# Reordering decodes, low parts, left sums and x differences at the end of the first block of a fused retention and two-layer kernel

## The chip, the cores and the metric

The kernel runs on one core of one Trainium2 chip. The metric is the device time of one execution in microseconds (us). The kernel before takes 845.2 us, the median of 3 runs (844.39 to 845.39).

## The reference

```python
def _attn_ref(q, k, v):                    # (4, 8, 576, 64) each
    scores = (1.0 / np.sqrt(D_)) * np.matmul(q, k.transpose(0, 1, 3, 2))
    Dmat = np.where(rel >= 0, gamma[:, None, None] ** rel[None, :, :], 0.0)
    return np.matmul(scores * Dmat[None, :, :, :], v)

x = attn_out.transpose(0, 2, 1, 3).reshape(B * S, H * D)      # 2304 x 512
h = x @ moe_w_in                                              # 512 x 2048
x = np.maximum(h, 0.0) ** 2 @ moe_w_out                       # 2048 x 512
h = x @ moe2_w_in
out = (h * np.clip(h + 3.0, 0.0, 6.0) / 6.0) @ moe2_w_out
```

The weights arrive as 64 bit floats. The kernel keeps close to float32 accuracy by splitting each operand into a rounded high part and a low part (the rest), and by doing three products (high by high, high by low, low by high) for one.

## The kernel before

**Stages.** The retention comes first (up to about 64 us). Then the first layer works on three blocks of 768 tokens and the second layer on three more. The first block of the first layer is special: it runs over 16 chunks of 128 hidden columns, loop `for c in range(NCH)` (L940), and on the way turns all the weights of layer 1 from 64 bit words to float32 and splits them. The five other blocks run as `NPAIR * len(BLOCKS)` = 40 pairs of chunks (L1022), in which `pair` (L675) makes the hidden part of two chunks with seven products of half size (P1 to P7, in the order P1, P6, P2, P7, P5, P4, P3; a Strassen scheme) in place of eight. The seven products take seven right operands, made of x and of differences of x, and left operands made of the weights and of sums of them.

**One chunk c of the first block** (L940 to L1003). TensorE does `emit_h(c)` (L423: 24 matmuls into PSUM banks 6 and 7), and at the chunk's end `firsts(c - 2)` (24 matmuls with the hidden values of two chunks ago). The other engines do, each in the order of the program:

- `decode` (L155) of one half of a weight chunk: two ScalarE passes (L171, L172, "first"), then VectorE's `clamp` (L175, L178), `second` (L184) and `third` (L190). In chunk c those of the output weights `wd` of chunk c-1 and of the input weights `w` of chunk c+2; in chunk 14 the two are the output weights of 13 and of 14.
- `emit_g(c)` (L459): ReLU, square and high part on ScalarE (L447, L450, L451) for both halves, then the two low parts on VectorE (L454).
- `split_out` (L404) and `split_in` (L395): high part on ScalarE (L196), low part on GpSimd (L197).
- in odd chunks `sum_lefts` (L936): the left sums of a pair, four VectorE subtractions and additions (L508 to L511), and their store, which is queued in `late_stores` and issued by `store_late` (L499) on SP.
- `next_load` (L769): the next load of weights, on SP, which waits until VectorE has read the old contents of its buffer (L184).

**The border to the pairs.** `operand_steps` (L568) gives three lists for the next block: `sums`, eight VectorE differences of x, two for each of T1, T2, T3 and T4 (L585); `highs` (L602, ScalarE) and `lows` (L607, VectorE), a high and a low part of each of the seven right operands. `parts_of_left` (L635) gives the high and low part of a left operand (L196 on ScalarE, L197 on VectorE), `load_left` (L613) loads one pair's left operands on SP. In the kernel before T1, T2, T3 stand at the end of chunks 11, 12, 13; `highs[0]` at the end of 13; `highs[1]`, `lows[0]` and two high parts of left operands at the end of 14; in chunk 15, ahead of `emit_g(15)`, `lows[1]`, two low parts of left operands and the last `sum_lefts`. After the loop come `highs[2]` to `lows[4]` (L1006 to L1011), the late stores, the stores of two output weights, and `load_left(1)`. T4 stands after P1 of the first pair (L1047), ahead of the addition `add(u2, tb, p1)` (L729; the instruction is L714), which must have read bank `b1` before P7 may write it (L735).

**Slots.** `ready_slots` (L527) spreads the decoding and splitting of layer 2's weights over 119 slots, which `between(i)` of the pairs takes one by one (L1060): seven per pair, none in the last pair of a block, three in the first pair of a later block. One period of 14 slots serves one pair of chunks: sums on GpSimd (L508 to L511) may go as soon as the decode in slot 6 is done, left operands are split in slots 8, 11, 14 and 17 (that of slot 11 is half as wide, 128x256).

Of the kernel before, what the change touches and what calls it, by code (L numbers as in the profile page):

```python
# [74 lines left out]
def retention_moe_moe2(ctx, tc, qk, qk_last, kv, w_in, w_out, w_in2, w_out2, consts, out):  # L75
# [6 lines left out]
    NCH = DFF // 128  # L82
# [694 lines left out]
    with tc.manual_schedule():  # L777
# [153 lines left out]
        def firsts(c):  # L931
            return ywork(wouts[c], g[c], c == 0, c == NCH - 1)

        left_lows = []

        def sum_lefts(p):  # L936
            whole = left_sums(*(first_in[p][:, e] for e in range(2)), nc.vector)[1]
# [2 lines left out]
        for c in range(NCH):  # L940
            mine, p = wins[c], c // 2
            h = emit_h(c)
            dec, due = due, []
            if c < 2:
                opening(c, h, dec)
                dec = []
            first = dec[:1]
            dec = dec[len(first):]
            for d in first:
                for f in d:  # L950
                    f()
                next_load()
            for d in dec:
                d.pop(0)()
            if c == NCH - 1:
                lows[1]()
                for f in left_lows:
                    f()
                sum_lefts(p)
            if c > 1:  # L960
                emit_g(c, h)
            for d in dec:
                for f in d:
                    f()
                next_load()
            if c in (2, 3):
                load()
            store_late()
            for n, w in ((c, mine), (c + 1, wins.get(c + 1))):
                if w is not None and (n != c or not c):  # L970
                    keep(("s", 0, n // 2, n % 2), w.rearrange("p a b n -> p (a b n)"), slice(n % 2, 2))
            if 2 <= c < NCH - 1:
                split_out(c - 1, nc.gpsimd)
            if c >= NCH - 2:
                split_out(c, nc.gpsimd)
            while halves and halves[0][0] <= c:
                due.append(decode(*halves.pop(0)[1:]))
            for d in due[:1]:
                d.pop(0)()
            if c and c + 2 < NCH:  # L980
                split_in(c + 2)
            if c % 2 and c < NCH - 1:
                sum_lefts(p)
            for d in due[1:]:
                d.pop(0)()
            if c >= LAG:
                for f in firsts(c - LAG):
                    f()
                keep(("o", 0, c - LAG), wouts[c - LAG].rearrange("p e n -> p (e n)"))
            if c == NCH - 5:  # L990
                load_left(0)
            if NCH - 5 <= c < NCH - 2:
                for f in sums[2 * (c - NCH + 5):][:2]:
                    f()
            if c == NCH - 3:
                highs[0]()
            if c == NCH - 2:
                highs[1]()
                lows[0]()
                for e in (2, 3):  # L1000
                    high, low = parts_of_left(0, e)
                    high()
                    left_lows.append(low)  # L1003
        assert not halves and not due
        pending = firsts(NCH - 2) + firsts(NCH - 1)
        highs[2]()  # L1006
# [1 line left out]
        lows[2]()  # L1008
        highs[4]()
        lows[3]()  # L1010
        lows[4]()  # L1011
        store_late()
        for c in (NCH - 2, NCH - 1):
            keep(("o", 0, c), wouts[c].rearrange("p e n -> p (e n)"))
# [7 lines left out]
        for k in range(total):  # L1022
# [20 lines left out]
            if p == 0:  # L1043
                if j:
                    side[0].append(lows[4])
                else:
                    side[0] += sums[6:]  # L1047
                for i, at in ((5, 1), (6, 3)):
                    side[at].append(highs[i])
                    side[at + 1].append(lows[i])  # L1050
            for i, e in ((4, 1), (6, 0)):
# [5 lines left out]
                    for n in range(2):  # L1057
                        side[i + n].append(lambda e=e, n=n: parts_of_left(k + 1, e)[n]())
            if p < NPAIR - 1:
                for i in range(4 if j and not p else 0, 7):  # L1060
                    if slots:
                        side[i] += [store_late] + slots.pop(0)
            elif late_stores:
# [54 lines left out]
```

## Time and profile before

| what | value |
|---|---|
| median of the runs | 845.2 us (844.39 to 845.39) |
| profiled execution, its own time | 845.26 us |
| span of the profiled execution | 843.5 us |
| TensorE (PE) busy | 825.0 us, 98% |
| VectorE (DVE) busy | 586.1 us, 69% |
| ScalarE (ACT) busy | 466.6 us, 55% |
| GpSimd (POOL) busy | 144.5 us, 17% |
| granted TensorE clock | 0.999, at the upper level throughout |

The span runs from the first to the last instruction; 1.76 us lie around it. A row of the timeline gives the start in us from the span's start, the duration in us, the engine, the line of the kernel, the operation, output and inputs, how many instructions are merged in the row, and in brackets the idle time of the engine before it with what ended it.

### The profile page before, as it was taken

The numbers are of one execution on the slowest core, as the hardware profiler recorded it, in microseconds if no ns is written. First come the engines' busy times: TensorE is split into PE (matmuls) and PEld (weight loads), VectorE is DVE, ScalarE is ACT, GpSimd is POOL, SyncE is SP. The second block draws the span as 40 slices with busy tenths as digits, with TensorE's granted clock in tenths as the row PEclk, the third lists the DMA queues.
The fourth block names the chain that finished last, engine by engine and source line by source line (L and its number), as shares of the span: only waits on it lengthen the run. The fifth ranks groups of instructions, "written<-read, shape, count | busy, mean of one in ns | idle before, by whom it ended". The sixth has DMA issues, their size and how long they took to land.

```text
span 843.5 us, 14173 instructions
## 1 busy us (share of the span) xinstructions
PE 825.0 (98%) x5220; PEld 741.9 (88%) x5220; DVE 586.1 (69%) x1018; ACT 466.6 (55%) x913; POOL 144.5 (17%) x122
## 2 busy tenths in 40 slices
PE   8989999997999999999999999999999999999998
PEld 7878888886999899999999888898898888889886
DVE  5779999999787876887875895546644546534434
ACT  1248777768865876867775653335433345433332
POOL 2353333331332320132230130000000000000000
PEclk9999999999999999999999999999999999999999
DMA  9996788876787894689786688553854552854522
GB/s 364 343 300 221 239 289 282 294 249 242 258 326 275 304 330 177 232 280 362 276 293 266 225 287 312 202 185 137 316 221 163 188 199 87 329 209 161 201 99 75
DMA packets 77963, 206.58 MB, mean 245 GB/s; under 512 B 8005, under 2 KB 24773, under 8 KB 77895
## 3 DMA queue, kind: packets, MB, share of 16 engines
q1 hardware_dynamic: 77314, 204.90, 68.9%
q8 instruction: 41, 0.67, 0.3%
q10 hardware_dynamic: 580, 0.79, 0.3%
q14 instruction: 28, 0.22, 0.1%
HBM read 159.00 MB, written 46.66 MB: 244 GB/s over the span
## 4 chain that ended last, share of the span: by engine, by line
PE 80%; DVE 7%; DMA 6%; ACT 4%; issue 1%; SPq 1%; POOL 0%; DVEq 0%; ACTq 0%; POOLq 0%
PE hps L690 33%; PE yps L650 22%; PE yps L478 13%; PE ytail L478 7%; PE hps L431 5%; DMA kvt<-in_kv_dram 3%; DMA qkt<-in_qk_dram 3%; DVE a L184 1%; DVE g L454 1%; DMA stage<-in_w_out_dram 1%; DVE w L190 1%; DVE a L178 1%; ACT u L706 0%; ACT r L172 0%; DVE u L714 0%
## 5 line engine op out<-in xcount | busy, mean ns | idle before, releaser
L650 PE MATMUL yps<-wo,g 128*128 128x512 f32 x864 | 226.8, 394 | 1.5 <-DVE g L710 1.3
L690 PE MATMUL hps<-xlast,win 128*128 128x384 f32 x960 | 194.9, 338 | 1.7 <-DVE u L714 1.6
L650 PEld LDWEIGHTS yps<-wo,g 128*128 128x128 f32 x864 | 159.4, 188 | 26.0 <-DVE g L710 2.0
L690 PEld LDWEIGHTS hps<-xlast,win 128*128 128x128 f32 x960 | 167.7, 188 | 10.5 <-DVE u L714 2.1
L714 DVE TENSOR_TENSOR u<-hps,u 128x384 f32<-128x384 f32 x120 | 66.8, 557 | 157.1 <-PE hps L690 150.5
L478 PE MATMUL yps<-g,wo 128*128 128x512 f32 x576 | 166.1, 396 | 0.4 <-POOL wo L197 0.4
L690 PE MATMUL hps<-xop,win 128*128 128x384 f32 x720 | 146.4, 338 | 3.7 <-ACT r L447 3.4
L690 PEld LDWEIGHTS hps<-xop,win 128*128 128x128 f32 x720 | 125.7, 188 | 10.7 <-ACT r L447 3.6
L708 ACT ACTIVATE g<-c 128x384 fp32r<-128x384 f32 x120 | 63.1, 525 | 88.1 <-DVE c L707 86.6
L478 PEld LDWEIGHTS yps<-g,wo 128*128 128x128 f32 x576 | 101.8, 188 | 10.2 <-POOL wo L197 0.8
L478 PEld LDWEIGHTS ytail<-g,wo 128*128 128x128 f32 x576 | 94.0, 188 | 17.3
L478 PE MATMUL ytail<-g,wo 128*128 128x256 f32 x576 | 98.5, 279 | 0.0
L710 DVE TENSOR_TENSOR g<-c,g 128x384 fp32r<-128x384 f32 x120 | 67.9, 566 | 11.3 <-ACT g L708 11.1
L431 PE MATMUL hps<-xring,win 128*128 128x512 f32 (+1 forms) x384 | 69.7, 338 | 0.3 <-ACT r L447 0.2
L733 ACT ACTIVATE c<-hps 128x384 f32<-128x384 f32 x40 | 19.7, 492 | 90.9 <-PE hps L690 90.9
L431 PEld LDWEIGHTS hps<-xring,win 128*128 128x128 f32 x384 | 60.1, 190 | 8.7 <-ACT r L447 0.7
L706 ACT ACTIVATE u<-c,three 128x384 f32<-128x384 f32 x72 | 44.4, 617 | 31.7 <-DVE c L714 30.5
L714 DVE TENSOR_TENSOR c<-hps,u 128x384 f32<-128x384 f32 x80 | 44.3, 554 | 21.8 <-PE hps L690 21.7
L184 DVE SCALAR_TENSOR_TENSOR a<-stage,a 128x512 int32<-128x512 int32 x64 | 51.2, 800 | 0.9
L707 DVE SCALAR_TENSOR_TENSOR c<-u,c 128x384 f32<-128x384 f32 x72 | 41.3, 574 | 13.5 <-ACT u L706 13.4
L171 ACT ACTIVATE a<-stage 128x512 f32<-128x512 f32 x64 | 42.4, 663 | 6.4 <-DMA stage<-in_w_in_dram 6.4
L172 ACT ACTIVATE r<-stage 128x512 int32<-128x512 uint32 x64 | 42.2, 660 | 0.0
(97 smaller groups left out, 905.5 us busy)
## 6 DMA issues: line engine op xcount, KB each, us to landing
win<-kept SPq DMA_DIRECT2D x88, 512.0 KB
wo<-kept SPq DMA_DIRECT2D x80, 512.0 KB
kept<-ready SPq DMA_DIRECT2D x40, 512.0 KB
win<-kept SPq DMA_DIRECT2D x72, 256.0 KB
stage<-in_w_out_dram SPq DMA_DIRECT2D x32, 512.0 KB
kept<-wo SPq DMA_DIRECT2D x16, 512.0 KB
stage<-in_w_in_dram SPq DMA_DIRECT2D x16, 512.0 KB
qkt<-in_qk_dram SPq DMA_DIRECT2D x13, 512.0 KB
```

Source lines behind the costliest of these rows:

```text
L171: nc.scalar.activation(out=a, in_=high.bitcast(F32), func=ACTF.Abs)
L172: nc.scalar.activation(out=r, in_=low.bitcast(U32), func=ACTF.Copy, scale=2.0 ** -29)
L184: nc.vector.scalar_tensor_tensor(out=a.bitcast(I32), in0=high, scalar=-0x40000000, in1=a.bitcast(I32), op0=ALU.bitwise_and, op1=ALU.bitwis ...
L431: nc.tensor.matmul(out=h, lhsT=w[:, kk // 2, wp, kk % 2 * 128:][:, :128], rhs=xs[kk][xp][:, o:o + n], start=m == 0, stop=m == 3 * KD - 1,)
L478: nc.tensor.matmul(out=p, lhsT=w[:, wp, m * 128:m * 128 + 128], rhs=gt[:, gpart, o:o + n], start=first and e == 0 and not (k and m % 2), s ...
L650: nc.tensor.matmul(out=p, lhsT=gt[:, gpart, m * 128:m * 128 + 128], rhs=w[:, wp], start=first and e == 0, stop=last and e == 2,)
L690: nc.tensor.matmul(out=to, lhsT=wl[k][:, half if k != 1 else 0, wp, o], rhs=x[:, xp, f], start=first and m == 0, stop=last and m == 5, ski ...
L706: nc.scalar.activation(out=v, in_=c, func=ACTF.Relu, bias=three)
L707: nc.vector.scalar_tensor_tensor(out=c, in0=v, scalar=6.0, in1=c, op0=ALU.min, op1=ALU.mult)
L708: nc.scalar.activation(out=hi, in_=c, func=ACTF.Copy)
L710: lambda: nc.vector.tensor_tensor(out=lo, in0=c, in1=hi.bitcast(F32), op=ALU.subtract)
L714: nc.vector.tensor_tensor(out=out_, in0=to, in1=x, op=ALU.add)
```

## The change

It moves work in the first block and at its border; nothing is added or left out.

- In chunk 14 the rest of the decode of the output weights of 14 (`second`, `third`) and the load behind it go ahead of `emit_g(14)`.
- In chunk 15 one low part of a left operand is left there (that of operand 2); the one of operand 3 and the last `sum_lefts` go behind `lows[4]`, after the loop, and its store with them. The high part of operand 3 goes behind `lows[3]`.
- In chunk 13 `highs[0]` goes ahead of `split_in(15)`.
- T1, T2, T3 go to the ends of chunks 4, 6 and 8.
- In the first pair T4 goes from after P1 to after P6 (behind the addition L729), `highs[5]` and `lows[5]` one place later, and the slots of that pair begin at its place 3 in place of 0, so that all later slots come three places later.

```diff
-        left_lows = []
...
+            if c == NCH - 2:
+                for d in dec:
+                    for f in d:
+                        f()
+                    next_load()
+                dec = []
             if c == NCH - 1:
                 lows[1]()
-                for f in left_lows:
-                    f()
-                sum_lefts(p)
+                left[0][1]()
             if c > 1:
                 emit_g(c, h)
...
+            if c == NCH - 3:
+                highs[0]()
             if c and c + 2 < NCH:
                 split_in(c + 2)
...
-            if NCH - 5 <= c < NCH - 2:
-                for f in sums[2 * (c - NCH + 5):][:2]:
+            if c in (4, 6, 8):
+                for f in sums[c - 4:][:2]:
                     f()
-            if c == NCH - 3:
-                highs[0]()
             if c == NCH - 2:
                 highs[1]()
                 lows[0]()
-                for e in (2, 3):
-                    high, low = parts_of_left(0, e)
-                    high()
-                    left_lows.append(low)
+                left = [parts_of_left(0, e) for e in (2, 3)]
+                left[0][0]()
...
         lows[3]()
+        left[1][0]()
         lows[4]()
+        left[1][1]()
+        sum_lefts(NPAIR - 1)
         store_late()
...
                 else:
-                    side[0] += sums[6:]
-                for i, at in ((5, 1), (6, 3)):
+                    side[1] += sums[6:]
+                for i, at in ((5, 1 if j else 2), (6, 3)):
...
-                for i in range(4 if j and not p else 0, 7):
+                for i in range(0 if p else 4 if j else 3, 7):
```

## Rows read from the trace of the kernel before

**Rows 1.** The page: busy time of the engines, and two of its costliest groups.

```profile
PE 825.0 (98%) x5220; PEld 741.9 (88%) x5220; DVE 586.1 (69%) x1018; ACT 466.6 (55%) x913; POOL 144.5 (17%) x122
...
L650 PE MATMUL yps<-wo,g 128*128 128x512 f32 x864 | 226.8, 394 | 1.5 <-DVE g L710 1.3
...
L710 DVE TENSOR_TENSOR g<-c,g 128x384 fp32r<-128x384 f32 x120 | 67.9, 566 | 11.3 <-ACT g L708 11.1
```

**Rows 2.** Timeline of TensorE, 155 to 215 us: the rows with idle time.

```profile
181.98 4.45 PE L431 MATMUL hps<-xring,win 128*128 128x512 f32 x24 [0.21 <-ACT r L447]
...
187.26 0.50 PE L478 MATMUL yps<-g,wo 128*128 128x512 f32 x1 [0.37 <-POOL wo L197]
...
194.70 1.31 PE L690 MATMUL hps<-xop,win 128*128 128x384 f32 x6 [3.43 <-ACT r L447]
...
203.27 1.32 PE L690 MATMUL hps<-xlast,win 128*128 128x384 f32 x6 [1.56 <-DVE u L714]
```

**Rows 3.** Timeline of ScalarE in chunks 14 and 15.

```profile
188.95 0.63 ACT L196 ACTIVATE wo<-wd 128x512 fp32r<-128x512 f32 x1 [3.62 <-DVE wd L190]
...
191.43 1.13 ACT L196 ACTIVATE win<-win 128x512 fp32r<-128x512 f32 x2
...
194.28 0.37 ACT L447 ACTIVATE r<-hps 128x256 f32<-128x256 f32 x1
```

**Rows 4.** Timeline of VectorE from chunk 14 to the first pair.

```profile
182.21 0.41 DVE L175 TENSOR_SCALAR a<-a 128x512 f32<-128x512 f32 x1
...
185.38 2.11 DVE L454 TENSOR_TENSOR g<-r,g 128x512 fp32r<-128x512 f32 x2
...
190.18 1.12 DVE L175 TENSOR_SCALAR a<-a 128x512 f32<-128x512 f32 x1 [0.32 <-ACT a L171]
...
201.73 1.01 DVE L585 TENSOR_TENSOR xall<-xall,t 128x384 f32<-128x384 f32 x2
202.67 0.55 DVE L714 TENSOR_TENSOR u<-hps,u 128x384 f32<-128x384 f32 x1
```

**Rows 5.** Timeline of VectorE: its first instruction of chunk 4 and of chunk 10.

```profile
95.71 0.41 DVE L175 TENSOR_SCALAR a<-a 128x512 f32<-128x512 f32 x1
...
145.81 0.42 DVE L175 TENSOR_SCALAR a<-a 128x512 f32<-128x512 f32 x1
```

**Rows 6.** Timeline of all engines, 153 to 158 us: a GpSimd operation and two L184.

```profile
153.23 1.31 POOL L197 TENSOR_TENSOR win<-w,win 128x512 fp32r<-128x512 f32 x1 [2.40 <-ACT win L196]
153.27 1.81 DVE L184 SCALAR_TENSOR_TENSOR a<-stage,a 128x512 int32<-128x512 int32 x1
...
157.63 0.69 DVE L184 SCALAR_TENSOR_TENSOR a<-stage,a 128x512 int32<-128x512 int32 x1
```

**Rows 7.** Timelines of TensorE (hidden matmuls of chunks 4, 10) and ScalarE (ReLU of 9).

```profile
89.43 4.34 PE L431 MATMUL hps<-xring,win 128*128 128x512 f32 x24
...
139.71 4.34 PE L431 MATMUL hps<-xring,win 128*128 128x512 f32 x24
...
137.46 0.59 ACT L447 ACTIVATE r<-hps 128x512 f32<-128x512 f32 x1
```

**Rows 8.** SP's and ScalarE's timelines at the first pair; DMA rates, 195 to 220 us.

```profile
198.09 0.32 SPq L412 DMA_DIRECT2D kept<-sums  x1
...
203.46 1.06 SPq L621 DMA_DIRECT2D win<-kept  x2
...
209.36 0.62 ACT L196 ACTIVATE win<-win 128x512 fp32r<-128x512 f32 x1
...
GB/s 0 26 13 0 0 0 315 413 406 406 393 419 400 393 197 302 354 252 318 400 216 315 360 387 406 426 419 419 419 403 390 403 390 370 356 218 39 0 26 0
```

**Rows 9.** Timeline of all engines in the second layer, around a wait of TensorE.

```profile
501.13 0.73 POOL L197 TENSOR_TENSOR ready<-wd,ready 128x256 fp32r<-128x256 f32 x1 [7.18 <-ACT ready L196]
501.17 1.10 DVE L710 TENSOR_TENSOR g<-c,g 128x384 fp32r<-128x384 f32 x1
...
502.32 0.73 PE L650 MATMUL yps<-wo,g 128*128 128x512 f32 x2 [0.97 <-DVE g L710]
```

## The prediction

> **What bounds the kernel now.** I read the page first: TensorE is busy for 98% of the span [rows 1], so a reordering can only win back what TensorE still waits. Its timeline comes next, for the rows with idle time [rows 2]. From 77 to 181 us there is none. Then come four: 0.21, 0.37, 3.43 and 1.56, together 5.57 us, at the first matmuls of chunk 15, at the output matmuls of chunk 13, at P1 of the first pair and at its P7. That is all that the border can give. The rows name the releasers: the ReLU of chunk 15 for P1, the addition L714 for P7. So the third view is what those two engines did before. ScalarE stood idle 3.62 us until the decode of the output weights of 14 was through, and only afterwards came to that ReLU at 194.28 [rows 3]. VectorE has next to no idle time from chunk 14 (182.21) to L714 (202.67): the largest is 0.32 [rows 4]. P7 therefore starts when VectorE has worked off its list, and P1's wait is a wait that P7 would have later anyhow.
>
> **Was VectorE full earlier, too?** This decides the moved differences of x. From chunk 4 to chunk 10 VectorE's start moves by 145.81 - 95.71 = 50.10 us in three periods of two chunks, 16.70 each [rows 5]. TensorE's start moves by 139.71 - 89.43 = 50.28, 16.76 each [rows 7]. From chunk 10 to 14 VectorE takes 182.21 - 145.81 = 36.40 [rows 4, 5], that is two periods and 3.0 more, and in between stand exactly T1, T2 and T3. One pair of differences costs 202.67 - 201.73 = 0.94 [rows 4], three 2.82. So each difference pushed VectorE back by its whole length: there was no gap to fill.
>
> A GpSimd operation is part of that list. L184 takes 0.69 alone and 1.81 when a GpSimd operation has started 0.04 ahead of it [rows 6]: 1.12 lost, four times in two chunks. The Trainium skill, SBUF — State Buffer, section "SBUF: two separate sides", has the two engines share a port pair as an exclusive lock, which whoever starts first holds for the whole instruction, against VectorE operations in a two-port mode or with two SBUF inputs; by it L184 would wait, as here, and an addition that reads PSUM would not. By that rule the lost time can't be ordered away, only handed from one instruction to another.
>
> **The change, part by part.**
>
> - *T1, T2, T3 to chunks 4, 6, 8.* VectorE regains 16.76 - 16.70 = 0.06 us per two chunks, some 0.2 from chunk 8 to 14. So it comes to chunk 14 at about 182.2 as before. I take 0 for this part; the bounds are 0 and -2.8 (if the chunks do hide the three). On the way VectorE is late by 0.94, 1.88, 2.82 us. The ReLU of chunk 9 ends at 137.46 + 0.59 = 138.05, and chunk 10's matmuls need that bank at 139.71 [rows 7]: 1.66 us in hand. TensorE would wait there, about 0.3 at the matmuls of chunk 10 and some 1.2 in all by chunk 12. These waits come out of the border's, since the end is VectorE's.
> - *The decode of 14 ahead of the low parts.* The two low parts take 2.11, of which 1.12 is the lock [rows 4, 6], which will now fall on the decode instead; so the decode ends 0.99 earlier. One high part of a left operand less ahead of the ReLU gives half of 1.13 [rows 3], 0.56. P1 can come at 194.70 - 1.55 = 193.15. VectorE's own list gets no shorter by it, except for the 0.32 that it waited for ScalarE [rows 4]. Against that, the GpSimd operation which overlapped that idle time cost 1.12 - 0.41 = 0.71 there [rows 4], and now has its full 1.12: +0.41.
> - *highs[0] ahead of split_in(15), last left sums and one left low part late.* They stay ahead of L714, so P7 sees the same sum; ScalarE does the high part while it waits for the weights. 0.
> - *T4 behind the addition.* The only work that leaves VectorE's list ahead of L714: -0.94. It is then ahead of the next addition, which needs P7 (1.2 us later) anyway; `highs[5]` and P4 come over 3 us later.
> - *The store of the last sums.* It is issued when the sums are done, some 4 us later than 198.09 [rows 8], and SP holds the output stores and `load_left(1)` behind it. Its third part was issued at 203.46 and is first read at 209.36 [rows 8]. From the store on, 2.5 MB are moved to the end of that part, 6.2 us at the 0.4 MB per us that the row of rates shows [rows 8]: landed at about 209.0, needed at 208.6. ScalarE would wait 0.4, and about 1 us there is covered by the low parts that VectorE has yet to do. 0, bounds 0 and +1.0. The Trainium skill, SBUF — State Buffer, section "The DMA setup-cost knee (why "@ 1 MiB" ≠ asymptote)", gives each transfer about 2 us on top of its bytes, mostly until completion is confirmed; by that the part lands at 211, ScalarE waits 2.4, and the sum would be higher by an estimated 1.4 less what VectorE covers. The rows here don't show a landing, so the sum goes without it.
> - *Slots three places later.* In the second layer VectorE works on the path between the pairs: TensorE waits there for L710 for 1.3 us in all [rows 1], 0.97 of it in one place, where L710 takes 1.10 because a GpSimd low part began 0.04 ahead of it [rows 9]; on average it takes 0.57 [rows 1]. Three places later, the slot that falls there holds the wide low part instead of the 128x256 one, with the four sums shortly before it. Whether L710 or GpSimd is first is a matter of 0.2 us. Bounds: -1.3 (both waits go) and +2.7 (four sums and the wider part each add 0.53, as 1.10 - 0.57). Nearest is the row of today, so 0.
>
> **The sum.** -0.94 - 0.32 + 0.41 = -0.85. The profiled execution has 845.26, its median is 845.2, so one count serves for both: 844.4. A measurement of this kernel can tell about 0.2% (1.7 us) from no change, so this is no difference.
>
> **The rivals.**
>
> *The chunks hide the three differences.* TensorE had no idle time in chunks 3 to 13 and 1.66 us in hand at the ReLU. If VectorE catches up (a lock that falls into idle time), it comes to chunk 14 2.8 us earlier, P1's wait goes altogether, and P7 gains 2.8 + 0.85 of the 5.57: 841.6. Against it stand 16.70 of 16.76 us and the 3.0 us above. 28%.
>
> *Slots collide with the low parts between the pairs of layer 2.* This one ends on the other side. Its place is the end of the first and third pair of the second layer; it decides when GpSimd's operation starts ahead of L710. At +2.7 from the bounds above, with the border's -0.85, it gives 847.1. For it: today's 0.97 with a narrower part. Against it: in the first layer the same slots stand at two other places of the pair with no wait of TensorE for L710, and a wider high part starts GpSimd 0.2 us later, behind L710. 20%.
>
> *P1 is released, P7 is not.* The change does what it says at P1 (1.55 earlier) and all of it comes back at P7. This is my forecast, 52%; its own range is 843.2 to 845.8 (T4 alone and the late loads at either end).
>
> **How the numbers follow.** Faster by over 0.2% (below 843.5): 0.25 of the first rival and 0.05 of the forecast's lower end, 0.30. Slower (above 846.9): 0.16 of the second, with 0.01 from late loads, 0.17. The rest, 0.53, is no difference. The range leaves out about half of the first rival, below 841.6, and the top of the second, above 847.0.
>
> **What would show it.** In the changed kernel's timeline: VectorE's start of chunk 14 at 182 (the first rival: at 179.5); new waits of TensorE by the matmuls of chunks 10 to 12, about 1.2 us; P1 at about 193.2; L714 and P7 at about 201.8 and 202.4, with a wait of over 2 us ahead of P7; two waits for L710 in the second layer, as now or longer. The forecast is wrong if P7 comes before 201, or if TensorE's waits after 210 us exceed 2.5.

## The result and the profile after

The changed kernel takes 850.96 us (median of 7 runs) where the kernel before takes 844.84 beside it: ratio 1.0075, 95% interval 1.0057 to 1.0092. It is 6.1 us slower; the forecast was 844.4.

The page of the changed kernel, busy time and the groups that wait (its profiled execution took 849.28 us, span 847.5):

```profile
PE 829.4 (98%) x5220; PEld 742.9 (88%) x5220; DVE 588.1 (69%) x1018; ACT 465.4 (55%) x913; POOL 141.7 (17%) x122
...
L650 PE MATMUL yps<-wo,g 128*128 128x512 f32 x864 | 227.3, 394 | 1.8 <-DVE g L710 0.8
...
L690 PE MATMUL hps<-xop,win 128*128 128x384 f32 x720 | 146.7, 338 | 4.8 <-ACT u L725 2.3
...
L710 DVE TENSOR_TENSOR g<-c,g 128x384 fp32r<-128x384 f32 x120 | 66.7, 555 | 11.5 <-ACT g L708 10.8
```

TensorE's waits for L710, which the forecast watched, went down from 1.3 [rows 1] to 0.8. In their place stand 2.3 us of waits for L725, the copy of a pair's first product, which the page of before doesn't have. And TensorE is busy 4.4 us longer with the same 5220 matmuls: some of the waiting is inside rows that count as busy. At 469.14 three output matmuls take 1.04 us, with a weight load that waits 0.29 for L710, and 0.86 without; and the clock fell, as shown below.

The timeline of TensorE, its rows with idle time around the border and in the first pairs of layer 2:

```profile
190.90 1.33 PE L690 MATMUL hps<-xop,win 128*128 128x384 f32 x6 [1.73 <-ACT r L447]
...
195.71 1.31 PE L690 MATMUL hps<-xop,win 128*128 128x384 f32 x6 [0.31 <-ACT u L725]
...
200.00 1.65 PE L690 MATMUL hps<-xlast,win 128*128 128x384 f32 x6 [1.93 <-DVE u L714]
...
474.03 1.31 PE L690 MATMUL hps<-xop,win 128*128 128x384 f32 x6 [1.01 <-ACT u L725]
...
487.42 0.73 PE L650 MATMUL yps<-wo,g 128*128 128x512 f32 x2 [0.35 <-DVE g L710]
...
502.72 1.31 PE L690 MATMUL hps<-xop,win 128*128 128x384 f32 x6 [0.64 <-DVE c L714]
...
504.58 0.49 PE L650 MATMUL yps<-wo,g 128*128 128x512 f32 x1 [0.55 <-ACT g L708]
...
505.56 0.73 PE L650 MATMUL yps<-wo,g 128*128 128x512 f32 x2 [0.48 <-DVE g L710]
...
509.17 1.33 PE L690 MATMUL hps<-xop,win 128*128 128x384 f32 x6 [0.45 <-ACT u L725]
```

P1 is at 190.90 and P7 at 200.00, both early on the clock of the page, but the first chunk's matmuls began at 61.33 here and at 63.82 before: attention took 2.5 us less in this one execution. So the border is read from that start on. P1: 129.57 now, 130.88 before. P7: 138.67 now, 139.45 before. The border gained 0.78 at P7, as forecast. From there on it was lost.

The timeline of VectorE (first instruction of chunks 4, 10 and 14, then the addition and T4, which changed places):

```profile
93.26 0.41 DVE L175 TENSOR_SCALAR a<-a 128x512 f32<-128x512 f32 x1
...
146.34 0.41 DVE L175 TENSOR_SCALAR a<-a 128x512 f32<-128x512 f32 x1
...
179.72 0.41 DVE L175 TENSOR_SCALAR a<-a 128x512 f32<-128x512 f32 x1
...
199.39 0.55 DVE L714 TENSOR_TENSOR u<-hps,u 128x384 f32<-128x384 f32 x1
199.86 1.02 DVE L585 TENSOR_TENSOR xall<-xall,t 128x384 f32<-128x384 f32 x2
```

Chunk 4 to 10 takes 53.08 us, where it took 50.10 [rows 5]: 2.98 more for the three differences. Chunk 10 to 14 takes 33.38, where it took 36.40 [rows 4, 5]. From 4 to 14 both kernels take 86.5. Moving the differences moved VectorE's delay and nothing else.

On the way TensorE was held, but not by the ReLU that the forecast named. What it waited for from 130 to 185 us (total, times, longest), where the kernel before has no such row:

```profile
PEld yps L478 <- POOL wo L197: 1.6, 4, 0.7
```

These are the weight loads of the output matmuls, which wait for GpSimd's low part of the output weights. That follows ScalarE's high part, which waits for the decode (L190) on the delayed VectorE.

The windows of five us behind P7's wait; PEclk is the last column but two:

```profile
195.00:200.00 5.00, 2.76 (x17) 2.22 (x15) 4.97 (x13) 1.15 (x3) 0.00 (x0) 1.00 0.00 0
200.00:205.00 5.00, 5.00 (x19) 4.69 (x20) 2.38 (x6) 3.88 (x8) 0.00 (x0) 0.66 0.95 343
205.00:210.00 5.00, 5.00 (x30) 4.60 (x29) 4.97 (x11) 3.54 (x7) 0.00 (x0) 1.00 0.97 323
```

After three waits (1.73, 0.31 and 1.93 us) the granted clock fell. TensorE was busy all of the second five us and did 19 matmuls in them; in the next five it did 30.

To find the 6 us I cut each profile into pieces that don't depend on when the first chunk started. The start of a pair is its first P1 matmul in TensorE's timeline; all are counted from the first chunk's first matmul. A pair without any wait takes 15.85 us in layer 1 (pairs 0 to 15; pair 16 too) and 15.69 in layer 2 (from pair 17 on). The table has all the profiles of this study, the experiments of the next section among them. The kernel before took 844.2 to 845.9 in the rounds that it ran beside the others, so the ratios are compared rather than the medians:

| profile | pair 2 starts at | pairs 2 to 16 | pairs 17 to 19 | median of its runs, ratio [95%] |
|---|---|---|---|---|
| before | 164.91 | 239.12 | 48.97 | 844.84 |
| before2 | 165.11 | 240.15 | 48.99 | one run |
| before3 | 164.92 | 240.48 | 49.14 | one run |
| after | 166.13 | 240.63 | 52.70 | 850.96, 1.0075 [1.0057, 1.0092] |
| after2 | 166.48 | 241.90 | 52.71 | one run |
| s0 | 166.05 | 239.78 | 49.05 | 846.01, 1.0025 [1.0014, 1.0037] |
| b3 | 164.90 | 240.78 | 52.72 | 849.51, 1.0069 [1.0057, 1.0082] |
| instep | 166.30 | 240.29 | 48.95 | 846.38, 1.0031 [1.0019, 1.0043] |
| nolow | 166.27 | 238.62 | 51.55 | 849.36, 1.0061 [1.0048, 1.0074] |
| store | 165.64 | 239.04 | 48.97 | 844.45, 1.0006 [0.9991, 1.0022] |
| sums3 | 164.85 | 238.78 | 48.99 | 844.63, 0.9999 [0.9988, 1.0010] |
| off1 | 166.02 | 248.26 | 48.01 | 855.63, 1.0131 [1.0113, 1.0150] |
| off4 | 166.08 | 238.50 | 51.93 | 847.79, 1.0048 [1.0028, 1.0068] |
| ph1 | 165.17 | 238.08 | 48.93 | 842.77, 0.9978 [0.9965, 0.9990] |
| t4 | 165.26 | 239.53 | 48.97 | 845.22, 1.0010 [0.9998, 1.0022] |
| s0_t11 | 166.22 | 239.29 | 48.96 | 845.01, 1.0010 [1.0000, 1.0019] |
| best | 163.78 | 238.09 | 48.93 | 842.23, 0.9972 [0.9962, 0.9981] |
| six5 | 166.06 | 249.84 | 55.83 | 861.80, 1.0184 [1.0157, 1.0211] |
| six0 | 164.94 | 238.63 | 50.90 | 846.74, 1.0019 [1.0007, 1.0030] |

After minus before, by the means of their profiles: border and first two pairs +1.3, pairs 2 to 16 +1.4, pairs 17 to 19 +3.7, together 6.3. The pieces behind pair 19 differ by up to 0.6 in either direction. Pairs 2 to 16 vary by over 1 us from one execution of the same kernel to another, pairs 17 to 19 by 0.2.

### The profile page after: what moved, and what is told of

Same layout as the page of the kernel before. It is cut to its first block, busy times and chain, and to the rows that moved or that the text cites. A ratio compares the mean times of both kernels' runs of the same rounds, so it can differ in the third digit from the quotient of the medians.

```text
span 847.5 us, 14184 instructions
## 1 busy us (share of the span) xinstructions
PE 829.4 (98%) x5220; PEld 742.9 (88%) x5220; DVE 588.1 (69%) x1018; ACT 465.4 (55%) x913; POOL 141.7 (17%) x122
## 4 chain that ended last, share of the span: by engine, by line
PE 53%; DVE 18%; DMA 12%; ACT 9%; issue 4%; POOL 1%; SPq 1%; DVEq 0%; ACTq 0%; POOLq 0%
PE hps L690 24%; PE yps L650 21%; PE yps L478 4%; DMA kept<-ready 4%; DMA kvt<-in_kv_dram 4%; DVE a L184 3%; DVE g L454 2%; PE ytail L478 2%; DVE wd L190 2%; DVE a L175 2%; DVE a L178 1%; DMA wo<-kept 1%; DMA win<-kept 1%; DVE w L190 1%; ACT ready L196 1%
## 5 line engine op out<-in xcount | busy, mean ns | idle before, releaser
L708 ACT ACTIVATE g<-c 128x384 fp32r<-128x384 f32 x120 | 63.0, 525 | 88.4 <-DVE c L707 86.9
L710 DVE TENSOR_TENSOR g<-c,g 128x384 fp32r<-128x384 f32 x120 | 66.7, 555 | 11.5 <-ACT g L708 10.8
L707 DVE SCALAR_TENSOR_TENSOR c<-u,c 128x384 f32<-128x384 f32 x72 | 42.2, 586 | 14.6 <-ACT u L706 14.4
L184 DVE SCALAR_TENSOR_TENSOR a<-stage,a 128x512 int32<-128x512 int32 x64 | 50.5, 789 | 0.8
L171 ACT ACTIVATE a<-stage 128x512 f32<-128x512 f32 x64 | 42.3, 661 | 5.9 <-DMA stage<-in_w_in_dram 5.9
L175 DVE TENSOR_SCALAR a<-a 128x512 f32<-128x512 f32 x64 | 40.5, 633 | 6.7 <-ACT a L171 6.6
```

The costliest lines, as they stand in the source:

```text
L171: nc.scalar.activation(out=a, in_=high.bitcast(F32), func=ACTF.Abs)
L175: nc.vector.tensor_scalar(out=a, in0=a, scalar1=LEAST, scalar2=MOST, op0=ALU.max, op1=ALU.min)
L184: nc.vector.scalar_tensor_tensor(out=a.bitcast(I32), in0=high, scalar=-0x40000000, in1=a.bitcast(I32), op0=ALU.bitwise_and, op1=ALU.bitwis ...
L707: nc.vector.scalar_tensor_tensor(out=c, in0=v, scalar=6.0, in1=c, op0=ALU.min, op1=ALU.mult)
L708: nc.scalar.activation(out=hi, in_=c, func=ACTF.Copy)
L710: lambda: nc.vector.tensor_tensor(out=lo, in0=c, in1=hi.bitcast(F32), op=ALU.subtract)
```

## The experiments

**The slots' place, alone and undone.** In s0 the changed kernel has the slots where they were; b3 is the kernel before with the slots' new place alone.

```
s0:  - range(0 if p else 4 if j else 3, 7)     + range(4 if j and not p else 0, 7)
b3:  the same line, the other way round, in the kernel before
```

> The kernel after with the slots of the first pair back at place 0; all other moves stay. Theory S (the slots' place costs the time, 5.7 us of it in the pairs): 844 to 845.5, not slower than before; pairs 1 to 20 take what they take before, P7 still about 0.8 earlier against the first chunk. Rival B (the border costs it: later stores and loads, a clock that falls after the waits): 850 to 851, as the kernel after.

> The kernel before with the slots of the first pair beginning at place 3; nothing else is moved. Theory S: 850 to 851, slower by 5 to 6 us, with the second layer's pairs 17 to 19 longer by 3.7 in all and the first layer's by about 2. Rival B: 845, as before.

s0 846.01, b3 849.51. The one line alone costs 5.3 us (849.51 against 844.20 beside it), and undoing it gives back 4.3 of the 6.1. Pairs 17 to 19 take 52.72 in b3 and 49.05 in s0. So most of the loss belongs to a line that I had costed at nothing, and it is made hundreds of us behind the border. s0 is still slower than before, by 1.8 (846.01 against the same 844.20).

**Which slots.** A slot's place in its pair is (slot + a constant) mod 7, with one constant for pairs 0 to 7, one for pairs 8 to 15 (the two blocks of layer 1 that run as pairs) and one for the first block of layer 2: 0, 4, 1 before, 3, 0, 4 after. In instep pair 8 takes six slots, which gives 3, 4, 1. off1 starts at place 1 (1, 5, 2), off4 at place 4 (4, 1, 5).

```
instep:  - range(0 if p else 4 if j else 3, 7)   + range(0 if p else (3, 1, 4, 4, 4)[j], 7)
off1:    - range(0 if p else 4 if j else 3, 7)   + range(0 if p else 4 if j else 1, 7)
off4:    - range(0 if p else 4 if j else 3, 7)   + range(0 if p else 4, 7)
```

> The kernel after, but the first pair of the third block takes six slots in place of three, so that from there on all slots stand where they stand before. Theory S: the first layer's second block keeps its 0.6 us, the rest goes: 845 to 846.5, pairs 17 to 19 as before (waits of 0.4 and 1.0). Rival B: 850 to 851.

> The kernel after with the first slot at place 1 in place of 3. In the second layer no slot with ScalarE's two decode passes then falls on place 6 (ahead of the copy of P1), and the sums start at place 1. Either theory of the second layer's waits (ScalarE's passes ahead of the copy, or GpSimd's hold on VectorE at a pair's end): pairs 17 to 19 take 49 to 50, as before, not 52.7; the time is 847 to 848.5. If it is the later start of the slots by itself, about a third of the 5 us: pairs 17 to 19 take 50.2.

> The kernel after with the first slot at place 4. In the second layer no slot with ScalarE's passes falls on place 6, but GpSimd's sums start at place 4 and the wide low part falls on place 6. If ScalarE's passes make the waits, pairs 17 to 19 take 49 to 50 and the time is 847 to 848.5; if GpSimd's hold on VectorE makes them, they take 52 or more and the time is 850 to 852.

With constant 1 in layer 2 (before, s0, instep) pairs 17 to 19 take 49.0, with 2 (off1) 48.0, with 4 (after, b3) 52.7, with 5 (off4) 51.9. So it isn't "later" that costs but the place. instep came out as expected from the place (846.38).

off1 is as cheap as expected in pairs 17 to 19 (48.0 for 49 to 50), but its time is a miss: 855.63 for 847 to 848.5. In layer 1 it is the same as in layer 2 with other values: constant 5 in pairs 8 to 15 makes off1 8 us slower there. Its waits of TensorE from 220 to 560 us (total, times, longest):

```profile
PE yps L478 <- DVE g L710: 9.1, 4, 2.5
PE yps L650 <- DVE g L710: 0.3, 1, 0.3
```

Four pairs of 18.3 to 19.0 us, each with 2.2 to 2.5 us of wait for L710 by the output matmuls of the layer that I had held to be safe.

off4 took what GpSimd's theory gave for pairs 17 to 19 (51.93 for "52 or more"); its time, 847.79, is in the range of the other theory, as pairs 2 to 16 took only 238.50. From 220 to 560 us TensorE doesn't wait for L725 in it, but twice for L710. That wait, and GpSimd and VectorE at the end of pair 16:

```profile
PE yps L650 <- DVE g L710: 3.3, 2, 1.7
...
466.15 0.93 POOL L509 TENSOR_TENSOR sums<-sums,wd 128x256 f32<-128x256 f32 x1
466.41 1.09 DVE L707 SCALAR_TENSOR_TENSOR c<-u,c 128x384 f32<-128x384 f32 x1
```

Constant 5 puts GpSimd's four sums at place 5, so they run at the end of every other pair. While they run, the L710 at 465.57 takes 0.91 instead of 0.55 and L707 1.09 instead of 0.56, and the next L710 comes too late for TensorE. off1 has the same picture in layer 1: around the start of pair 9 the sums run from 340.03 to 343.84, L710 takes 0.92, the slot's L175 and L178 take 0.95 and 0.83 instead of 0.41 and 0.43, and TensorE waits until 345.12. So the collision of the second rival exists, at another constant than the forecast's.

**GpSimd's low parts left out.** nolow is the changed kernel in which GpSimd writes zeros for the low parts of layer 2's left operands instead of subtracting (hi, lo and src stand for the views of `split_left`).

```
-  split_to(hi, lo, src, nc.gpsimd)
+  split_parts(hi, lo, src, nc.gpsimd)[0]()
+  nc.gpsimd.memset(lo, 0.0)
```

> The kernel after, in which GpSimd writes zeros in place of the second layer's low parts of left operands (these low parts are left out). If GpSimd's hold on VectorE in those slots makes the waits of the second layer, the 3.7 us lost in pairs 17 to 19 shrink to about 1.5: 848 to 849. If ScalarE makes them (its two decode passes stand ahead of the copy of P1), the waits for that copy of 1.0 and 0.45 us stay and the time stays within 1 us of 851.

Pairs 17 to 19 fall from 52.70 to 51.55: 1.15 of the 3.7. That lies between the two theories (1.5 left, or none gone), and so does the time, 849.36: the wait for L725 at the start of pair 17 goes down from 1.01 to 0.67, the one of 0.45 goes. GpSimd's low parts are a part of the loss and not the most; its sums still run. What else there is shows in the chain that ends in the wait at 474.03. The timelines of GpSimd, VectorE and ScalarE in the changed kernel, from the end of pair 16 to the product P2 of pair 17:

```profile
466.70 0.56 DVE L707 SCALAR_TENSOR_TENSOR c<-u,c 128x384 f32<-128x384 f32 x1 [0.28 <-ACT u L706]
...
468.90 1.64 POOL L197 TENSOR_TENSOR ready<-wd,ready 128x512 fp32r<-128x512 f32 x1 [24.99 <-ACT ready L196]
...
469.67 1.29 DVE L707 SCALAR_TENSOR_TENSOR c<-u,c 128x384 f32<-128x384 f32 x1 [0.28 <-ACT u L706]
...
471.00 0.53 ACT L708 ACTIVATE g<-c 128x384 fp32r<-128x384 f32 x1 [1.36 <-DVE c L707]
...
472.38 0.66 ACT L171 ACTIVATE a<-stage 128x512 f32<-128x512 f32 x1
472.94 0.66 ACT L172 ACTIVATE r<-stage 128x512 int32<-128x512 uint32 x1
...
473.50 0.48 ACT L725 ACTIVATE u<-hps 128x384 f32<-128x384 f32 x1
```

L707 takes 0.56 alone and 1.29 behind the start of GpSimd's L197: 0.73 lost. L708 waits for it, and behind L708 ScalarE has two copies of outputs and then the slot of place 6, the unpacking of the next weights (L171 and L172, 1.2 us), ahead of L725. P2 goes on in the bank that L725 reads, so TensorE waits for 1.01 us.

**The slot of place 6 elsewhere.** This tells the two holders apart. six5 runs that slot at place 5, six0 at place 0 of the next pair, behind L725.

```
six5:  -  side[i] += [store_late] + slots.pop(0)
       +  side[min(i, 5)] += [store_late] + slots.pop(0)
six0:  +  side[0] += carried
       +  carried = []
       ...
       -  side[i] += [store_late] + slots.pop(0)
       +  to = carried if i == 6 else side[i]
       +  to += [store_late] + slots.pop(0)
```

> The changed kernel, with the slots of place 6 (the last of a pair) run at place 5 behind that place's own slot, so that none of a slot's work stands between a pair's last product and the copy at line 725 of the next pair; every other slot keeps its place. Theory two holders: in pairs 17 to 19 the slots' 3.73 us over the kernel before are partly ScalarE's, whose two unpacking instructions (lines 171 and 172, 1.2 us) at place 6 stand ahead of the next pair's copy at line 725 (PE waits 1.01 and 0.45 us there, with what they push), and partly VectorE's, held by GpSimd's low parts (1.15 us, measured by leaving them out). Then the waits for line 725 go, pairs 17 to 19 fall from 52.70 to about 51.3 us, the pairs of layer 1 lose the 0.3 us of theirs, and the time is 849 us, ratio 1.0055. Rival theory GpSimd alone: the waits for line 725 are only the last sign of a late VectorE; pairs 17 to 19 stay within 0.3 us of 52.7 or grow, as two slots now fall on one place: 851 us or more.

> The changed kernel, with the slots of place 6 run at place 0 of the next pair ahead of that place's own slot, so behind the copy at line 725 in ScalarE's order instead of ahead of it, and far from the next pair's end; every other slot keeps its place. Running them at place 5 cost 11 us, by waits for line 710 (12.8 us) in place of those for line 725, so a pair's end has no room on VectorE; its start has, if the slots of place 0 are as cheap as they were. Theory two holders: the waits for line 725 (1.01 and 0.45 us in pairs 17 to 19) go and nothing comes for them; pairs 17 to 19 fall from 52.70 to 51.3 us and the time to 849.3 us, ratio 1.0055. Rival theory no room: two slots at one place hold VectorE or ScalarE wherever they stand; the waits for line 725 go, others for lines 710 and 714 come, and the time is 851 us or more.

six5 misses the first theory's 849 and goes far beyond the 851 of the second: 861.8 us, some 10 more than the changed kernel. TensorE's waits in it, 220 to 560 us:

```profile
PE yps L478 <- DVE g L710: 8.3, 7, 3.1
PE yps L650 <- DVE g L710: 4.5, 3, 1.8
PE yps L650 <- ACT g L708: 0.8, 2, 0.5
PE hps L690 <- DVE c L714: 0.6, 1, 0.6
PE yps L478 <- ACT g L708: 0.3, 1, 0.3
```

L725 is gone from the list, but 12.8 us of waits for L710 came. The granted clock fell in it as well, behind the waits of 3.1 and 1.8 us (0.66 on average from 445 to 450 us, 0.75 from 515 to 520), in its two longest pairs (21.23 and 19.99). Two slots at place 5 are too much for the end of a pair, so this run doesn't tell the two holders apart. In six0 the same instructions stand where there is room:

```profile
PE yps L650 <- DVE g L710: 0.8, 2, 0.5
PE hps L690 <- DVE c L714: 0.6, 1, 0.6
PE yps L650 <- ACT g L708: 0.5, 1, 0.5
PE yps L478 <- DMA wo<-kept: 0.4, 1, 0.4
```

The waits for L725 are gone and nothing but 0.4 for a load came in their place. Pairs 17 to 19 take 50.90 (1.8 less, expected 1.4), pairs 2 to 16 take 238.63 (2.0 less than in the changed kernel's first profile, of which over 1 is within what one kernel varies there), the median is 846.74, lower than the 849.3 expected. So the slot of place 6 ahead of L725 is half of the loss in layer 2. At the end of pair 16 L707 takes 1.29 in six0 too, but L725 now comes ahead of L171 and L172. VectorE's step of that slot (L190) went behind L710 as well, and no run parts the two; the waits that went are ScalarE's. The waits that stay are those in which VectorE is late.

**The late store of the last sums.** s0 has the border's new order alone, and its pair 1 takes 17.84 us instead of 15.85. SP's timeline in s0:

```profile
187.89 1.13 SPq L412 DMA_DIRECT2D kept<-wo  x1
202.12 0.32 SPq L412 DMA_DIRECT2D kept<-sums  x1
202.53 1.22 SPq L412 DMA_DIRECT2D kept<-wo  x2
203.80 2.40 SPq L629 DMA_DIRECT2D win<-kept  x2
206.24 0.99 SPq L621 DMA_DIRECT2D win<-kept  x2
```

ScalarE's, at the high part of the operand that the last of them loads:

```profile
211.12 0.63 ACT L196 ACTIVATE win<-win 128x512 fp32r<-128x512 f32 x1 [1.47 <-DMA win<-kept]
```

TensorE's, behind it:

```profile
213.98 0.94 PE L478 MATMUL yps<-g,wo 128*128 128x512 f32 x3 [0.56 <-DMA wo<-kept]
...
218.31 1.33 PE L690 MATMUL hps<-xop,win 128*128 128x384 f32 x6 [0.95 <-ACT u L725]
```

Between the output stores (187.89) and the store of the sums SP issues nothing for 13 us, since the store waits for VectorE's last sum (L511) at the head of the queue. Both of the next kernels start from s0. In `store` the call stands behind the second pair's loads; in `sums3` the sums themselves are computed at place 3 of the first pair.

```
store:   sum_lefts(NPAIR - 1)                   sums3:  - sum_lefts(NPAIR - 1)
       - store_late()                                     store_late()
         ...                                              ...
         load_left(1)                                     side[1] += sums[6:]
       + store_late()                                   + side[3].append(lambda: sum_lefts(NPAIR - 1))
```

> The kernel s0 (all border moves, slots at place 0) with one change: the store of the last left sums is issued behind load_left(1), not ahead of the two output stores and of that load. If the 2.0 us that s0 loses in pair 1 come from these loads landing late, pair 1 takes 15.85 again, ScalarE does not wait for the left operand, and the time is 843.3 to 844, 0.85 under the kernel before. If they come from the slots or from T4 in the first pair, it stays at 846.

> The kernel s0 with the last left sums at place 3 of the first pair, behind P7's addition, their store with them. If VectorE's list sets P7, it starts 1.5 earlier than in s0 against the first chunk, and with the loads early as in the kernel before, pair 1 takes 15.85: 841.5 to 843, the fastest. If ScalarE or the loads set P7, it stays where s0 has it and the time is 844 or more.

`store`: pair 1 takes 15.85 again, without a wait, so the late loads are what s0 lost there. The median is that of before (844.45 against 844.97), not the 843.3 to 844 expected: in its profile the clock fell at P7, pair 0 took 20.22 instead of s0's 18.67, and pair 2 starts at 165.64, where before has 164.9 to 165.1. SP's timeline in it:

```profile
195.01 1.25 SPq L629 DMA_DIRECT2D win<-kept  x2
200.40 0.80 SPq L621 DMA_DIRECT2D win<-kept  x2
201.24 0.43 SPq L412 DMA_DIRECT2D kept<-sums  x1
```

The last of the loads goes out at 200.40 instead of 206.24, ahead of the store. sums3 starts pair 1 at 147.60 (before 149.06), since the four sums no longer stand ahead of P7's addition, but gives most of it back: the loads at L621 overwrite what the sums read, so they now wait for the sums, go out at 204.81, and pair 1 takes 17.25. It is a miss: 844.63 for 841.5 to 843.

**The moved differences, each way.** t4 is the kernel before with T4 late and nothing else; s0_t11 is s0 with T1 to T3 back in chunks 11 to 13.

```
t4:      - side[0] += sums[6:]                        + side[1] += sums[6:]
         - for i, at in ((5, 1), (6, 3)):             + for i, at in ((5, 1 if j else 2), (6, 3)):
s0_t11:  - if c in (4, 6, 8):                         + if NCH - 5 <= c < NCH - 2:
         -     for f in sums[c - 4:][:2]:             +     for f in sums[2 * (c - NCH + 5):][:2]:
```

> The kernel before with nothing changed but T4 (the last difference of x), computed behind the first pair's second product instead of ahead of it, and its high part a place later. The forecast's own first term alone: product P7 starts 0.94 us earlier, pair 1 starts 148.1 us behind the first chunk instead of 149.06, and the pairs behind it are as before: 843.9 us, ratio 0.999. Rival: the 0.94 us comes back within the first pair, where products P4 and P3 then wait for T4's parts or for VectorE: pair 1 starts at 149 again, 844.8 us.

> The changed kernel with the slots where they were before, and the differences T1 to T3 back in chunks 11, 12 and 13. Theory VectorE is full: chunk 15 starts 118.16 us behind the first chunk as before (with the differences early 119.25), but VectorE has the same work ahead of the first pair's product P7, so pair 1 starts within 0.3 us of 148.2 as with the differences early, and the time is 846.0 us, ratio 1.0025. Rival: the 1.1 us that the chunks lost is a loss of its own: pair 1 starts at 147.1, 844.9 us.

s0_t11: chunk 15 starts at 117.79 instead of s0's 119.25, and pair 1 at 148.25 instead of 148.21. The chunks' loss is no loss of its own; VectorE comes to P7 at the same time. The median, 845.01, is nearer to the rival's 844.9 than to 846.0. Its interval and that of s0 overlap, and no stretch of the two traces has that difference; but these are one profile each, with the clock falling at P1 in s0_t11 and nowhere in s0, so a loss of up to 1 us by the moved differences isn't excluded.

t4 is a miss: pair 1 starts at 149.41, later than before. VectorE does come to the addition 0.94 us earlier (137.91 from the first chunk, before 138.85), but TensorE doesn't use it: the clock fell at the end of P1's wait. The windows of t4:

```profile
192.00:194.00 2.00, 0.00 (x0) 0.00 (x0) 2.00 (x4) 1.92 (x4) 0.00 (x0) 0.75 0.00 0
194.00:196.00 2.00, 1.97 (x6) 1.97 (x7) 1.97 (x5) 1.96 (x5) 0.52 (x1) 0.50 0.06 12
```

**Whether the clock belongs to the kernel.** The same two kernels were profiled again, without an edit.

> The kernel before once more, for its profile alone. In its first profile the granted clock stayed at 1.00 through the border although PE waits 3.43 us for the first pair's product P1; in three kernels whose work up to that product is the same as its own, or nearly (slots moved by three, slots from place 1, T4 late), the clock fell to 0.50 behind that wait. Theory execution: the fall belongs to the single execution, not to the kernel, so it can show here too: at P1 six products of the pair and the chunk take 2.3 us instead of 1.3, the wait of P7 (1.56 us) shrinks to 0.5 or nothing, and pair 0 lasts 18.2 to 18.5 us all the same. Rival theory kernel: 1.00 throughout, the wait of P7 1.56 us and pair 0 18.18 us again.

> The kernel before a third time, for its profile alone, with the same two theories: by the theory execution a fall of the clock at the first pair shows in some of its profiles and in others not; by the theory kernel all three profiles stay at 1.00 there, with 1.56 us of wait at P7 and 18.18 us for pair 0.

> The changed kernel once more, for its profile alone. In its first profile the clock fell to 0.50 from about 201 to 204 us, behind waits of 1.73, 0.31 and 1.93 us, and pair 0 lasted 20.22 us and pair 1 16.34. Theory execution: without the fall it gives pair 0 18.7 us and pair 1 17.8, as the same order of the border did in the kernel with the slots at their old place; the slots' pairs 17 to 19 are 52.7 us in either case. Rival theory kernel: the fall comes again at the same product, with 20.2 us for pair 0.

before2, TensorE's timeline at P1:

```profile
193.69 2.29 PE L690 MATMUL hps<-xop,win 128*128 128x384 f32 x6 [3.44 <-ACT r L447]
```

before3, at P1 and at P7:

```profile
195.13 2.29 PE L690 MATMUL hps<-xop,win 128*128 128x384 f32 x6 [3.44 <-ACT r L447]
...
203.69 1.32 PE L690 MATMUL hps<-xlast,win 128*128 128x384 f32 x6 [0.42 <-DVE u L714]
```

Six matmuls in 2.29 us, where the first profile has 1.31 [rows 2]: the kernel before falls to 0.50 as well, in two of its three profiles, and pair 0 still takes 18.37 and 18.18 us. What the clock takes at P1 comes out of the wait at P7 (0.42 or none instead of 1.56). after2 falls at P7 like after, with 20.22 us for pair 0 again.

**A version that beats both.** ph1 is the kernel before with the slots at constant 1 in all three blocks. `best` is the changed kernel with that line, and with the last sums at place 1 of the first pair.

```
ph1:   - range(4 if j and not p else 0, 7)        + range(0 if p or j else 1, 7)
best:  - range(0 if p else 4 if j else 3, 7)      + range(0 if p or j else 1, 7)
       - sum_lefts(NPAIR - 1)
       - store_late()
         side[1] += sums[6:]
       + side[1].append(lambda: sum_lefts(NPAIR - 1))
```

> The kernel before with nothing changed but the slots' place: the first slot stands at place 1 of the first pair, and no slot is skipped later, so that slot s stands at place (s + 1) mod 7 of all three blocks that decode (before: places s, s + 4 and s + 1). Theory position: what a slot costs hangs on the place it stands at, and (s + 1) is the place that cost nothing beyond the shortest pairs in the runs so far. Pairs 5 and 9 fall from 16.98 and 16.05 us to 15.85, pairs 17 to 19 stay at 16.3, 15.7 and 17.0: 843.5 us, ratio 0.9985. Rival theory order: what costs is any slot that comes earlier than in the kernel before, through loads and tiles that are not ready, whatever its place: pairs of layer 1 with 0.5 to 1 us more as in the kernel with the slots alone moved by three, 846 us or more.

> The changed kernel with two things altered: the last left sums are computed and stored at place 1 of the first pair, behind the difference T4, instead of ahead of the pair and ahead of the second pair's loads; and the slots stand at place (s + 1) mod 7 of all blocks. If the border is worth what was read (VectorE reaches P7 0.85 us earlier by the reorder and 0.6 more without the sums ahead of it), the late loads cost nothing once the store is out of their way, and the slots' cost is one of position: pair 1 starts 147.6 us behind the first chunk (before 149.06) and lasts 15.85, pairs 5 and 9 fall by 1.1 and 0.2 us: 842.0 us, ratio 0.9965. Rival: the sums at place 1 put off the second pair's loads of the same tiles, as they did at place 3 (17.25 us for pair 1), and the slots' gain is not there: 844.5 us or more.

ph1 is faster than before, 842.77 at 0.9978 [0.9965, 0.9990]: pair 5 falls from 16.98 to 15.85 as expected, pair 9 stays at 16.12 (expected 15.85). `best` is 842.23 at 0.9972 [0.9962, 0.9981], for 842.0 expected; pair 1 starts at 146.88, earlier than the 147.6 expected, and takes 16.90 instead of 15.85. By the traces it has ph1's gain from the slots (pairs 2 to 16 take 238.1 in both, 1.0 to 2.4 less than in the profiles of before) and 1.1 from the border (pair 2 starts at 163.78); by the times the two can't be told apart.

## Why the prediction was wrong

By its own steps:

- *What bounds the border*: right. P7 starts when VectorE has worked off its list. Forecast 138.60 us behind the first chunk (202.42 less 63.82), measured 138.67; P1 129.33 and 129.57.
- *T1 to T3 moved, 0*: right at P7. The chunks lost 1.16 us more up to chunk 15 (about 1.2 forecast), though by waits for GpSimd's L197 and not for the ReLU, and in s0_t11's profile VectorE comes to P7 no earlier. The first rival, chunks that hide the differences, fell: 53.08 against 50.10 us.
- *T4, -0.94, and the sum of -0.85 at the border*: right in VectorE's list and, where the clock stayed up, in TensorE's: pair 1 starts at 148.21 in s0, 0.85 ahead of before.
- *The store of the last sums, 0 with an upper bound of 1.0*: wrong. Pair 1 took 2.0 more in s0. The step that failed is the landing: 6.2 us from the store on at the row's rate, measured 9.0 (202.12 to 211.12). The forecast's 209.0 doesn't even follow from it: a store at 202.1 and 6.2 us give 208.3. The Trainium skill, SBUF — State Buffer, section "The DMA setup-cost knee (why "@ 1 MiB" ≠ asymptote)", which I quoted and didn't count, puts some 2 us on top of each transfer's bytes; by that it would be an estimated 8.2, the nearer number. Nor did I ask what comes behind: the operand's high part stands in ScalarE's order ahead of what the next pair needs, and the late output weights cost 0.56 by themselves.
- *Slots three places later, 0 with bounds -1.3 and +2.7*: wrong, and the main part. It costs 5.3 us alone, 3.7 of them in pairs 17 to 19. "Nearest is the row of today, so 0" took one kind of wait (L710) at one place and let it stand for a slot at any place. A slot is ScalarE's unpacking, VectorE's arithmetic and GpSimd's low part, and each has a place of the pair where somebody is waited for. The waits for L710 did go down. The new ones are for L725, behind unpacking that now fell on place 6; the bounds had been made from L710 alone and couldn't hold them.
- *The second rival* had the side and the stretch (the first pairs of layer 2), but not the size or the holder: 3.7 us instead of 2.7, and only 1.15 by GpSimd's low parts. Its sign came: TensorE's waits after 210 us add up to 4.9, where 2.5 was the limit. "In the first layer the same slots stand at two other places with no wait" was true of the places 0 and 4; off1 pays 8 us in that layer.
- *The clock* had no place in the forecast, because the one profile shown of before kept it at 1.00. In that kernel the fall mostly comes where P7's wait absorbs it. The new order shortens P1's wait to 1.73 and puts the fall, where it comes, behind P7's, where nothing absorbs it: pair 0 takes 20.2 instead of 18.7. Where the loads are late it costs little in the sum, as TensorE would have waited for them anyhow: pairs 0 and 1 take 36.56 us with the fall (after) and 36.52 without (s0). In `store`, where they are early, it isn't covered: pair 0 takes 20.22 us, 1.55 more than in s0, and pair 1 is at its shortest, 15.85.
- *The range of the forecast*, 843.2 to 845.8, doesn't come out of its own terms: T4 alone gives 844.3, and the late loads, at their bound of 1.0, 845.4.

So the border brings P7 forward by 0.8 as forecast, but neither the changed kernel nor `store` shows that gain in its time: behind P7 the late loads took it, and with the store behind the loads (`store`, ratio 1.0006 [0.9991, 1.0022]) its one profile lost it to the clock. The one line on the slots cost six times the 0.85.

What stays open: how the rest of pairs 17 to 19 (1.9 us in six0) divides between GpSimd's operations and VectorE's own slot work in the changed kernel; and why the fall of the clock comes in one execution and not in another.

## What to carry to other kernels

Background work that is dealt out over the places of a loop has to be costed place by place and engine by engine: lay each of its instructions against the one that is waited for next on that engine, over the whole loop, since a shift by a few places moves all of it at once. Try the shifts by themselves; here they make 842.8 to 849.5 us of the kernel before and 846.0 to 855.6 of the changed one. And a store that waits for a late result belongs behind the loads where one queue issues both in order, as SP does here.

## What the runs showed of the hardware

The granted clock fell to 0.50 (1.2 GHz) at the border in 12 of 19 profiles: in six at P1 after a wait of 2.6 to 3.4 us, in six at P7 after waits of 1.7, 0.3 and 1.9 us. Executions of one kernel differ in it, before having one without and two with; and four kernels with those three waits kept 1.00 there (s0, nolow, six5, six0).

GpSimd holds more than L184: L707, with both its inputs in SBUF, took 1.29 us behind GpSimd's start instead of 0.56. That agrees with the Trainium skill, SBUF — State Buffer, section "SBUF: two separate sides", by which VectorE operations with two SBUF inputs wait for the lock.
